# Attention and mixture of depths on one core: VectorE adds GpSimd's partial sum of probabilities, with another order of stores, PSUM banks and first halves

## The chip, the core and the metric

The kernel runs on one core of a Trainium2 chip. The metric is device time in microseconds (us), the median of several executions; smaller is better. The engines of the core work side by side, each on its own queue of instructions: TensorE (PE: matmuls and transposes, its weight loads are PEld), VectorE (DVE), ScalarE (ACT), GpSimd (POOL) and SyncE (SP, which here only issues transfers). TensorE writes to PSUM, which has eight banks.

## What is computed

Two blocks follow each other, all in float32:

```python
# attention: batch 8, 12 heads, 448 tokens, 64 per head
q_n, k_n = (rmsnorm(q, g_q), rmsnorm(k, g_k))      # x / sqrt(mean(x*x) + 1e-6) * g
scores = (1 / sqrt(64)) * matmul(q_n, k_n.T)
attn = exp(scores - max(scores))
attn = attn / (sum(attn) + 1e-9)
x = matmul(attn, v)                                # then (8, 448, 12*64 = 768)

# mixture of depths, per batch b
scores = x[b] @ w_gate
top_idx = the 128 tokens with the highest scores
h = maximum(x[b, top_idx] @ w1, 0)                 # 768 -> 1024
ye = h @ w2                                        # 1024 -> 768
out[b] = x[b]; out[b, top_idx] += sigmoid(scores[top_idx])[:, None] * ye
```

## The kernel before

The 12 heads of a batch are worked off in 3 groups of 4, so there are 24 groups `n`, numbered over all batches. A group has two pairs of heads (`hh`) and two heads in each (`c`), and its keys come in NI = 7 blocks of 64; one block of one group is a unit `u`, of which there are 168. Scores are kept with the keys on the partitions, so that the sum over keys (the denominator of the softmax) is a sum over partitions and blocks.

The start: the array of TensorE is kept at work by transposes that nobody reads, while the first rows are squared (ScalarE), summed (VectorE) and raised to -1/2 (GpSimd).

```python
    ps = ps_moe.tile([128, 512], F32, tag="moe", name="warm_ps")
    for _ in range(26):
        nc.tensor.transpose(out=ps[:, 0:128], in_=ident, identity=ident)
    ...
    def sum_squares(n, i, sq):                     # i = 0: queries, 1: keys
        ss = sss.pop((n, i))
        for h in [slice(0, 1), slice(1, 2)] if (n, i) == (0, 0) else [slice(0, 2)]:
            nc.vector.tensor_reduce(out=ss[:, h], in_=sq[:, h], axis=AX.X, op=OP.add)
        rinv = norm_pool.tile([128, 2, NI], F32, name="rinv", bufs=8)
        nc.gpsimd.tensor_tensor(out=rinv, in0=ss, in1=neg_half, op=OP.pow)   # shapes cut
```

For groups 0 and 1 TensorE spreads the queries' factors over the partitions (28 small matmuls, `scale_q_early`), and VectorE multiplies the queries `qT` by them. For later groups the factors go to DRAM and come back as a row for all partitions:

```python
    def rows_out(n): ...   # rows (DRAM) <- rinv, SyncE's queue
    def rows_in(n): ...    # bc <- rows, two transfers on SyncE's queue
    def scale_q(n):        # qT = qT * gg * bc
        nc.vector.scalar_tensor_tensor(out=t, in0=t, scalar=gg, in1=bcs.pop(n), ...)
```

For each unit TensorE makes the scores in two banks out of four (`ps_sc`), ScalarE takes the exponential into `p`, and TensorE multiplies by the values into `av`. The sum of `p` over the blocks of a group is shared out, for the first two batches (n < 6, `by_pool`):

```python
    def add_probs(u):
        n, i = divmod(u, NI)
        if i == NI - 1 and sums_last(n):           # block 6 is left for TensorE
            lasts.setdefault(n, []).append(probs.pop(u))
            return
        first = 2 if by_pool(n) else 0
        if first and i == 1:                       # blocks 0 and 1: GpSimd
            t = first_tokens[n % 2]...
            nc.gpsimd.tensor_tensor(out=t, in0=probs.pop(u - 1), in1=probs.pop(u), op=OP.add)
            lasts[n] = [t]
        elif i > first:                            # blocks 2 to 5: VectorE
            ...
            nc.vector.tensor_tensor(out=sums[n], in0=... , in1=probs.pop(u), op=OP.add)

    def sum_keys(n):
        ps = aux([128, 512], "den_ps")
        terms = [sums.pop(n)] + lasts.pop(n, [])   # n < 6: sum, GpSimd's sum, block 6
        for t in terms:
            for hh in range(2):
                for odd in range(2):
                    nc.tensor.matmul(out=ps[...], lhsT=pick_pair, rhs=..., start=..., stop=...)
```

`invert_sums` transposes the denominators and VectorE takes their reciprocal (`rden`); `to_tokens` transposes the result (`x_ps`) and VectorE multiplies by `rden` into `x`. After the third group of a batch come the gates, the store of `x`, and the ranks of the tokens:

```python
    def score_rows(b):
        ps = aux([128, 512], "row_ps")             # aux: one bank, which den_ps and x_ps use too
        for j in range(NJ):
            nc.tensor.transpose(out=ps[...], in_=t[:, j, :], identity=...)
        nc.scalar.copy(out=rows, in_=ps[:CP, 0:S])
```

```python
        at(s, gate, n)                             # in last_tokens; a slot s is one unit
        at(s, store_x, b)                          # out <- x, 1344 KB, SyncE's queue
        at(s + 1, spread, b)
        ...                                        # in ranks_of
        at(s + 2, select, b)                       # selected (DRAM) <- x, GpSimd's queue
        at(s + 8 if s >= 0 else s + 3, load_selected, b)   # xe <- selected, SyncE's queue
```

The two layers of batch b (`moe_ps`, on the 128 selected tokens `xe`) are then worked off between the units of later groups. A transfer waits at its place in SyncE's queue until what it needs is there, and those behind it wait too.

Of the kernel before, what the change touches and what calls it, by code (L numbers as in the profile page):

```python
# [10 lines left out]
F32 = mybir.dt.float32  # L11
I32 = mybir.dt.int32
AF = mybir.ActivationFunctionType
OP = mybir.AluOpType
# [11 lines left out]
class Loads:  # L26
# [37 lines left out]
    def get(self, name, n, i=None):  # L64
        return self.tiles[name, n, i]
# [3 lines left out]
def fast(  # L69
# [21 lines left out]
    nc = tc.nc  # L91

    B, NP, _, S = loads.src["qT"].shape
    CP = 112
    NJ = S // CP
    D = 64
    NI = S // D
# [14 lines left out]
    norm_pool = ctx.enter_context(tc.tile_pool(name="norm", bufs=2))  # L112
# [7 lines left out]
    ps_sc = ctx.enter_context(tc.tile_pool(name="ps_sc", bufs=4, space=PSUM))  # L120
# [6 lines left out]
    def aux(shape, name):  # L127

        if PER * now[0] >= units:
            return ps_sc.tile(shape, F32, tag="sc", name=name)  # L130
        if spare[0]:
            return ps_moe.tile(shape, F32, tag="moe", name=name)
        return ps_aux.tile(shape, F32, tag="aux", name=name)
# [7 lines left out]
    load, get, neg_half = loads.load, loads.get, loads.neg_half  # L141

    ident = const.tile([128, 128], F32, name="ident")
# [12 lines left out]
    for c in range(2):  # L156
        nc.vector.memset(pick_pair[D * c : D * (c + 1), c : c + 1], 1.0)
    nc.vector.scalar_tensor_tensor(
        out=gg, in0=loads.gcol[:, 0:1], scalar=scale, in1=loads.gcol[:, 1:2], op0=OP.mult, op1=OP.mult
    )  # L160

    ps = ps_moe.tile([128, 512], F32, tag="moe", name="warm_ps")
    for _ in range(26):
        nc.tensor.transpose(out=ps[:, 0:128], in_=ident, identity=ident)  # L164

    wg = const.tile([CP, DM], F32, name="wg")
# [43 lines left out]

    def sum_squares(n, i, sq):
        ss = sss.pop((n, i))
        for h in [slice(0, 1), slice(1, 2)] if (n, i) == (0, 0) else [slice(0, 2)]:
            nc.vector.tensor_reduce(out=ss[:, h], in_=sq[:, h], axis=AX.X, op=OP.add)  # L214
        rinv = norm_pool.tile([128, 2, NI], F32, name="rinv", bufs=8)
        flat = "p h i -> p (h i)"
        nc.gpsimd.tensor_tensor(  # L217
            out=rinv.rearrange(flat),
            in0=ss.rearrange(flat),
            in1=neg_half.to_broadcast([128, 2 * NI]),  # L220
            op=OP.pow,
        )
        rinvs[n, i] = rinv

    def rows_out(n):
# [26 lines left out]
    def scale_q_early(n):  # L252

        rinv = rinvs.pop((n, 0))
        for c in range(2):
            ps = ps_sc.tile([128, 512], F32, tag="sc", name="sc")
            r = slice(D * c, D * (c + 1))
            for i in range(NI):
                for hh in range(2):
                    nc.tensor.matmul(  # L260
                        out=ps[D * hh : D * (hh + 1), D * i : D * (i + 1)],
                        lhsT=rinv[r, hh, i : i + 1].to_broadcast([D, D]),
                        rhs=ident[r, r],
                        start=True,
                        stop=True,
                    )
            t = get("qT", n)[:, c].rearrange("d (p i) -> d p i", i=NI)
            nc.vector.scalar_tensor_tensor(  # L268
                out=t,
                in0=t,  # L270
                scalar=gg,
                in1=ps[:, 0:S].rearrange("d (i p) -> d p i", i=NI),
                op0=OP.mult,
                op1=OP.mult,
            )
# [3 lines left out]
    probs, sums, avs, xTs, rdens, xs = {}, {}, {}, {}, {}, {}  # L279
# [41 lines left out]
    def add_probs(u):  # L321
        n, i = divmod(u, NI)
        if i == NI - 1 and sums_last(n):
# [3 lines that stand above are left out]
        if first and i == 1:  # L327
            t = first_tokens[n % 2].rearrange("p h i d -> p h (i d)")
            nc.gpsimd.tensor_tensor(out=t, in0=probs.pop(u - 1), in1=probs.pop(u), op=OP.add)
            lasts[n] = [t]  # L330
        elif i > first:
            begins = i == first + 1
            if begins:
                sums[n] = p_pool.tile([128, 2, S], F32, name="sum", bufs=2)
            nc.vector.tensor_tensor(  # L335
                out=sums[n], in0=probs.pop(u - 1) if begins else sums[n], in1=probs.pop(u), op=OP.add
            )

    def values_out(n):
        for c in (1, 0):  # L340
            t = norm_pool.tile([128, NJ, CP], F32, name="xT", bufs=4)
            nc.scalar.copy(out=t.rearrange("d j p -> d (j p)"), in_=avs[n][c][:, 0:S])
            xTs[n, c] = t
        avs.pop(n)

    dens, lasts = {}, {}

    first_tokens = [get("tok", 0, i) for i in range(2)]

    def sums_last(n):  # L350


        return n < 2 * NG or n == n_groups - 1

    def by_pool(n):

        return n < 2 * NG
# [41 lines left out]
    def to_tokens(n, c):  # L399
        b = n // NG  # L400
        if b not in xs:
            xs[b] = x_pool.tile([CP, NJ, DX], F32, name="x")
        t = xTs.pop((n, c))
        shape = [128, NJ, 128]
        if c == 1 and not before_layers(now[0]):
            ps = ps_sc.tile(shape, F32, tag="sc", name="x_ps")
        else:
            ps = aux(shape, "x_ps")
        for j in range(NJ):
            nc.tensor.transpose(out=ps[:CP, j, :], in_=t[:, j, :], identity=ident)  # L410
        col = (n % NG * 2 + c) * 128
        nc.vector.tensor_tensor(  # L412
            out=xs[b][:, :, col : col + 128].rearrange("p j (h d) -> p j h d", d=D),
            in0=ps[:CP].rearrange("p j (h d) -> p j h d", d=D),
            in1=rdens[n][:, :, :, c, None].to_broadcast([CP, NJ, 2, D]),
            op=OP.mult,
        )
# [42 lines left out]

    def score_rows(b):
        t = rowss[b]
        ps = aux([128, 512], "row_ps")
        for j in range(NJ):
            nc.tensor.transpose(
                out=ps[:CP, CP * j : CP * (j + 1)], in_=t[:, j, :], identity=ident[:CP, :CP]
            )
        rows = moe_pool.tile([CP, S], F32, name="score_rows")
        nc.scalar.copy(out=rows, in_=ps[:CP, 0:S])
        nc.scalar.activation(out=parts[b], in_=parts[b], func=AF.Exp)  # L470
        rowss[b] = rows
# [162 lines left out]
    def at(slot, fn, *args):  # L634
        todo.setdefault(slot, []).append(lambda: fn(*args))

    now = [0, 0]
# [29 lines left out]
    for n in range(1, n_groups):  # L667
# [4 lines left out]
        if n > 1:  # L672
# [3 lines left out]
            first = max(s0 - (20 if n > 5 else 17), 0)  # L676
# [7 lines left out]
    def finish(n, q):  # L684

        if n == n_groups - 1:
            for fn, args in ((sum_keys, (n,)), (invert_sums, (n,)), (to_tokens, (n, 0))):
                task((q, 1), fn, *args)
            task((q, 1), last_tokens, n)
            return  # L690
        task((q, 1), sum_keys, n)
        task((q + 1, 0), to_tokens, n, 0)
        task((q + 1, 1), last_tokens, n)
# [7 lines left out]
    def before_layers(q):  # L701
        return done == 0 and ready.get(0, q + 1) > q

    def soon():

        q, place = now
        return PER * q + 2 * place if PER * q < units else -9

    def last_tokens(n):
        to_tokens(n, 1)  # L710
        b, g = divmod(n, NG)
        s = soon()
        at(s, gate, n)
        if g < NG - 1:
            return
        at(s, store_x, b)
        at(s + 1, spread, b)
        q, place = now

        when = (q + 1 + place // 2, 0) if b < B - 1 else (q + 1, 1)  # L720
        tasks.insert(0, (when, lambda: ranks_of(b)))

    def ranks_of(b):
        score_rows(b)
        s = soon()
        at(s, count, b, (0, 1))
        at(s + 1, count, b, (2, 3))
        at(s + 2, annotate, b)
        at(s + 2, select, b)
        at(s + 8 if s >= 0 else s + 3, load_selected, b)  # L730
        ready[b] = max((s + 8) // PER + 1, first_ff(b) - 1 if b else 0) if b < B - 1 else 0

    def first_ff(b):


        return -(-(units + 2 * PER - NG * NI * (B - 2 - b)) // PER)

    def run_values(upto, q):
        ended = False
        while waiting and waiting[0] <= upto:  # L740
            u = waiting[0]
            if ended and u % NI == 0:

                return
            values(waiting.pop(0))
            if u % NI == NI - 1:
                values_out(u // NI)
                finish(u // NI, q)
                ended = True
            add_probs(u)  # L750

    for i in range(2):
        sum_squares(0, i, squares(0, i))
    later = [squares(1, i) for i in range(2)]
    scale_q_early(0)
    for i in range(2):
        sum_squares(1, i, later[i])
# [587 lines left out]
```

## Time and profile before

| what | value |
|---|---|
| time, median of 3 runs | 530.28 us (528.81 to 530.87) |
| span of the profiled execution | 526.9 us |
| scores, 1344 matmul records | 154.8 us, 549 ns each |
| values, 1344 matmul records | 147.1 us, 537 ns each |
| denominators on GpSimd's sum (`den_ps<-tok`), 48 records | 3.4 us, 352 ns each |
| `sum<-sum,p` on VectorE, 128x896, 101 | 111.6 us, 1105 ns each |
| GpSimd's sum (`tok<-p`), 6 | 12.9 us, 2145 ns each |
| GpSimd's pow (`rinv<-ss`), 128x14, 48 | 128.8 us, 2689 ns each |
| out_dram<-x, 8 stores | 1344 KB each, 7.8 us from issue to landing (median) |

Records of matmuls overlap each other, up to four 64x64 parts of the array working at once, so the sums of their durations say less than the distance from one start to the next. A matmul of the program has two records. The wait view sums, for each instruction, the idle time of its engine just before it and names what ended it; the timeline lists instructions by start.

### The profile page before, as it was taken

To read this page: it belongs to the slowest core of one execution; us is meant where nothing else is said; L and a number is where in the kernel's file an instruction comes from. 1 tells how busy PE (TensorE), PEld (TensorE's weight loads), DVE (VectorE), ACT (ScalarE), POOL (GpSimd) and SP (SyncE) were. 2 spreads that over 40 slices of the span, in tenths; PEclk is the share of its full clock that TensorE was granted. 3 is DMA by queue.
4 is the path that set the end of the run, shared out by engine and by line. 5 is a ranking of instruction groups with operands and counts; after the bars stand their busy time and mean duration, and the time that the engine had idled before them with its cause. 6 is when DMAs were issued, how large, how long until landed. Compare 5 with 4: busy or idle time off the path is not lost.

```text
span 526.9 us, 11121 instructions
## 1 busy us (share of the span) xinstructions
PE 507.6 (96%) x4482; PEld 298.8 (57%) x4482; DVE 334.2 (63%) x638; ACT 278.1 (53%) x507; POOL 191.8 (36%) x109
## 2 busy tenths in 40 slices
PE   6999997999999999999999999998999999999995
PEld 5544343565744476546654467644664448659694
DVE  4566879579846896658666787467947487336101
ACT  4886873857644845456644585645463474401100
POOL 4956866623512454132712424304621003002102
PEclk9999998999999999999999999999999999999998
DMA  8968779799764297526846396537542231104100
GB/s 304 382 217 291 244 224 345 251 291 340 200 187 161 82 291 232 163 94 192 260 136 183 87 297 211 159 103 223 195 131 71 70 136 31 31 1 143 53 32 35
DMA packets 43405, 93.21 MB, mean 177 GB/s; under 512 B 11059, under 2 KB 23348, under 8 KB 43346
## 3 DMA queue, kind: packets, MB, share of 16 engines
q1 hardware_dynamic: 39938, 86.11, 52.1%
q0 software_dynamic: 3264, 6.31, 3.5%
q8 instruction: 37, 0.61, 0.5%
q14 instruction: 22, 0.18, 0.1%
q10 hardware_dynamic: 144, 0.00, 0.0%
HBM read 74.93 MB, written 25.35 MB: 190 GB/s over the span
## 4 chain that ended last, share of the span: by engine, by line
PE 89%; DVE 4%; DMA 2%; ACT 2%; issue 2%; POOL 0%; DVEq 0%; SPq 0%; ACTq 0%; POOLq 0%
PE sc L289 24%; PE av L313 22%; PE moe_ps L575 13%; PE moe_ps L595 11%; PE sc L595 4%; PE x_ps L410 4%; PE sc L575 4%; PE den_ps L367 3%; DMA bc<-rows 2%; PE denT_ps L392 1%; ACT p L298 1%; DVE sum L335 1%; PE warm_ps L164 1%; DVE ss L214 1%; DVE x L412 1%
## 5 line engine op out<-in xcount | busy, mean ns | idle before, releaser
L298 ACT ACTIVATE p<-sc,rinv 128x448 f32<-128x448 f32 x336 | 186.6, 642 | 106.3 <-PE sc L289 92.5
L217 POOL TENSOR_TENSOR rinv<-ss,neg_half 128x14 f32<-128x14 f32 x48 | 128.8, 2689 | 198.3 <-DVE ss L214 170.6
L289 PE MATMUL sc<-qT,kT 64*64 64x448 f32 x1344 | 154.8, 549 | 1.1 <-DVE qT L268 0.4
L313 PE MATMUL av<-p,v 64*64 64x448 f32 x1344 | 147.1, 537 | 0.0
L335 DVE TENSOR_TENSOR sum<-sum,p 128x896 f32<-128x896 f32 x101 | 111.6, 1105 | 7.2 <-ACT p L298 0.9
L313 PEld LDWEIGHTS av<-p,v 64*64 64x64 f32 x1344 | 60.1, 133 | 67.6 <-issue 56.9
L289 PEld LDWEIGHTS sc<-qT,kT 64*64 64x64 f32 x1344 | 54.3, 133 | 70.9 <-issue 47.0
L214 DVE TENSOR_REDUCE ss<-sq 128x14 f32<-128x910 f32 (+1 forms) x49 | 52.4, 1074 | 33.9 <-ACT sq L207 33.9
L575 PE MATMUL moe_ps<-xeT,w 128*128 128x128 f32 x576 | 69.3, 277 | 0.0
L575 PEld LDWEIGHTS moe_ps<-xeT,w 128*128 128x128 f32 x576 | 66.2, 192 | 5.3 <-issue 5.3
L595 PE MATMUL moe_ps<-w,hT 128*128 128x384 f32 x176 | 61.3, 491 | 0.4 <-DVE xe L604 0.3
L412 DVE TENSOR_TENSOR x<-x_ps,rden 112x512 f32<-112x512 f32 x48 | 32.8, 690 | 37.2 <-PE x_ps L410 36.4
L506 POOL DMA_INDIRECT selected<-x,rank x32 | 33.6, 1050 | 47.3 <-DVE x L498 39.3
L207 ACT ACTIVATE sq<-tok 128x896 f32<-128x896 f32 (+1 forms) x49 | 46.4, 951 | 5.7 <-DMA tok<-in_tok_dram 3.7
L595 PEld LDWEIGHTS moe_ps<-w,hT 128*128 128x128 f32 x176 | 31.7, 190 | 22.5 <-issue 2.5
L436 DVE SCALAR_TENSOR_TENSOR prod<-x,wg 112x256 f32<-112x256 f32 x96 | 41.5, 432 | 3.0
L614 POOL DMA_INDIRECT out_dram<-xe,row x10 | 11.6, 1164 | 81.1 <-DVE rden L394 47.3
L410 PE MATMUL x_ps<-ident,xT 128*112 128x128 f32 x192 | 29.5, 279 | 3.3 <-DVE rden L394 3.3
L335 DVE TENSOR_TENSOR sum<-p 128x896 f32<-128x896 f32 x24 | 25.9, 1078 | 5.2 <-ACT p L298 5.2
L604 DVE SCALAR_TENSOR_TENSOR xe<-sc,xe 128x384 f32<-128x384 f32 (+1 forms) x6 | 3.3, 550 | 40.6 <-PE sc L595 40.6
L410 PEld LDWEIGHTS x_ps<-ident,xT 128*112 128x112 f32 x192 | 21.8, 135 | 12.6 <-issue 7.7
L248 DVE SCALAR_TENSOR_TENSOR qT<-qT,gg,bc 128x896 f32<-128x896 f32 x22 | 25.2, 1147 | 5.1 <-DMA bc<-rows 5.1
(71 smaller groups left out, 311.0 us busy)
## 6 DMA issues: line engine op xcount, KB each, us to landing
tok<-in_tok_dram SPq DMA_DIRECT2D x48, 448.0 KB, 6.3
qT<-in_qT_dram SPq DMA_DIRECT2D x24, 448.0 KB, 6.2
kT<-in_kT_dram SPq DMA_DIRECT2D x24, 448.0 KB, 7.0
v<-in_vp_dram SPq DMA_DIRECT2D x24, 448.0 KB, 7.7
out_dram<-x SPq DMA_DIRECT2D x8, 1344.0 KB, 7.8
bc<-rows SPq DMA_DIRECT2D x44, 224.0 KB, 6.4
xe<-selected SPq DMA_DIRECT2D x8, 385.0 KB, 3.1
w<-in_moe_w_dram SPq DMA_DIRECT2D x6, 512.0 KB, 6.4
```

The source lines that it names most:

```text
L207: nc.scalar.activation(out=sq[:, h, :, 0:D], in_=t[:, h], func=AF.Square, scale=scale)
L214: nc.vector.tensor_reduce(out=ss[:, h], in_=sq[:, h], axis=AX.X, op=OP.add)
L217: nc.gpsimd.tensor_tensor(out=rinv.rearrange(flat), in0=ss.rearrange(flat), in1=neg_half.to_broadcast([128, 2 * NI]), op=OP.pow,)
L289: nc.tensor.matmul(out=scs[hh][D * c : D * (c + 1), 0:S], lhsT=get("kT", n)[r, c, D * i : D * (i + 1)], rhs=get("qT", n)[r, c, :], start=True,
L298: nc.scalar.activation(out=p[:, hh], in_=scs[hh][:, 0:S], func=AF.Exp, scale=rinvs[n, 1][:, hh, i : i + 1],)
L313: nc.tensor.matmul(out=avs[n][c][D * hh : D * (hh + 1), 0:S], lhsT=get("v", n)[r, hh, i, :], rhs=probs[u][r, hh], start=(i == 0), stop=(i ...
L335: nc.vector.tensor_tensor(out=sums[n], in0=probs.pop(u - 1) if begins else sums[n], in1=probs.pop(u), op=OP.add)
L410: nc.tensor.transpose(out=ps[:CP, j, :], in_=t[:, j, :], identity=ident)
L412: nc.vector.tensor_tensor(out=xs[b][:, :, col : col + 128].rearrange("p j (h d) -> p j h d", d=D), in0=ps[:CP].rearrange("p j (h d) -> p j ...
L436: nc.vector.scalar_tensor_tensor(out=prod, in0=xs[b][:, j, cols], scalar=1.0, in1=wg[:, cols], op0=OP.mult, op1=OP.mult, accum_out=gates[b ...
L575: nc.tensor.matmul(out=ps[:, 128 * i : 128 * i + n], lhsT=w1[:, dc, 128 * (f0 + i) : 128 * (f0 + i + 1)], rhs=xeT[:, dc, :n], start=(dc == 0),
L595: nc.tensor.matmul(out=ps[:n, :width], lhsT=hT[:, fc, :n], rhs=w2[:, fc, cols], start=(fc == 0), stop=(fc == NFC - 1),)
```

## The change

It has five parts.

- The transposes at the start are 13 instead of 26; for the first group the pow is taken by halves (one `hh` at a time), and the spreading matmuls go through both heads `c` of the first half before the second, so that they can begin with half of the factors.
- The sum that GpSimd makes of blocks 0 and 1 is added to `sums` by VectorE, after block 5, and TensorE no longer multiplies it into the denominators. It is meant to take work off TensorE.
- The score rows take a bank of the four of the scores instead of the one that they share with the denominators, once the layers have begun.
- The store of `x` is issued four units later, so that the row broadcasts and loads of later groups stand ahead of it in SyncE's queue.
- The load of the selected tokens is issued three units later, for the same reason.

```diff
-    for _ in range(26):
+    for _ in range(13):
         nc.tensor.transpose(out=ps[:, 0:128], in_=ident, identity=ident)
...
+        rinv = norm_pool.tile([128, 2, NI], F32, name="rinv", bufs=8)
         for h in [slice(0, 1), slice(1, 2)] if (n, i) == (0, 0) else [slice(0, 2)]:
             nc.vector.tensor_reduce(out=ss[:, h], in_=sq[:, h], axis=AX.X, op=OP.add)
-        rinv = norm_pool.tile([128, 2, NI], F32, name="rinv", bufs=8)
-        nc.gpsimd.tensor_tensor(out=rinv..., in0=ss..., in1=neg_half..., op=OP.pow)
+            nc.gpsimd.tensor_tensor(out=rinv[:, h]..., in0=ss[:, h]..., in1=neg_half..., op=OP.pow)
...  scale_q_early
-        for c in range(2):
-            ps = ps_sc.tile([128, 512], F32, tag="sc", name="sc")
-            for i in range(NI):
-                for hh in range(2):
-                    nc.tensor.matmul(out=ps[...], lhsT=rinv[r, hh, i : i + 1]..., rhs=ident[r, r], ...)
+        spreads = [ps_sc.tile([128, 512], F32, tag="sc", name="sc") for _ in range(2)]
+        for hh in range(2):
+            for c, i in [(c, i) for i in range(NI) for c in range(2)]:
+                nc.tensor.matmul(out=spreads[c][...], lhsT=rinv[r, hh, i : i + 1]..., rhs=ident[r, r], ...)
...  add_probs
-            lasts[n] = [t]
+            firsts[n] = t
...
+            if first and i == NI - 2:
+                nc.vector.tensor_tensor(out=sums[n], in0=sums[n], in1=firsts.pop(n), op=OP.add)
...  score_rows
-        ps = aux([128, 512], "row_ps")
+        if before_layers(now[0]):
+            ps = aux([128, 512], "row_ps")
+        else:
+            ps = ps_sc.tile([128, 512], F32, tag="sc", name="row_ps")
...
-        at(s, store_x, b)
+        at(s + 4 if s >= 0 else s, store_x, b)
...
-        at(s + 8 if s >= 0 else s + 3, load_selected, b)
+        at(s + 11 if s >= 0 else s + 3, load_selected, b)
```

More of the change, by code (lines that the diff above doesn't have):

```diff
@@ L212, in sum_squares @@
         ss = sss.pop((n, i))
+        rinv = norm_pool.tile([128, 2, NI], F32, name="rinv", bufs=8)
+        flat = "p h i -> p (h i)"
         for h in [slice(0, 1), slice(1, 2)] if (n, i) == (0, 0) else [slice(0, 2)]:
             nc.vector.tensor_reduce(out=ss[:, h], in_=sq[:, h], axis=AX.X, op=OP.add)
-        rinv = norm_pool.tile([128, 2, NI], F32, name="rinv", bufs=8)
[L216 to L222, printed above, removed]
+            nc.gpsimd.tensor_tensor(
+                out=rinv[:, h].rearrange(flat),
+                in0=ss[:, h].rearrange(flat),
+                in1=neg_half.to_broadcast([128, (h.stop - h.start) * NI]),
+                op=OP.pow,
+            )
         rinvs[n, i] = rinv
@@ L254, in scale_q_early @@
         rinv = rinvs.pop((n, 0))
-        for c in range(2):
-            ps = ps_sc.tile([128, 512], F32, tag="sc", name="sc")
-            r = slice(D * c, D * (c + 1))
-            for i in range(NI):
-                for hh in range(2):
[L260 to L266, printed above, removed]
+        spreads = [ps_sc.tile([128, 512], F32, tag="sc", name="sc") for _ in range(2)]
+        for hh in range(2):
+            for c, i in [(c, i) for i in range(NI) for c in range(2)]:
+                r = slice(D * c, D * (c + 1))
+                nc.tensor.matmul(
+                    out=spreads[c][D * hh : D * (hh + 1), D * i : D * (i + 1)],
+                    lhsT=rinv[r, hh, i : i + 1].to_broadcast([D, D]),
+                    rhs=ident[r, r],
+                    start=True,
+                    stop=True,
+                )
+        for c in range(2):
             t = get("qT", n)[:, c].rearrange("d (p i) -> d p i", i=NI)
@@ L271, in scale_q_early @@
                 scalar=gg,
-                in1=ps[:, 0:S].rearrange("d (i p) -> d p i", i=NI),
+                in1=spreads[c][:, 0:S].rearrange("d (i p) -> d p i", i=NI),
                 op0=OP.mult,
@@ L344, in values_out @@
         avs.pop(n)
-    dens, lasts = {}, {}
+    dens, lasts, firsts = {}, {}, {}
     first_tokens = [get("tok", 0, i) for i in range(2)]
```

## The prediction

> **What bounds the kernel now.** I read first the busy times of the page, then the idle time of TensorE by what ended it, then the stretches in which that idle time lies, in order of time.
>
> ```profile
> span 526.9 us, 11121 instructions
> PE 507.6 (96%) x4482; PEld 298.8 (57%) x4482; DVE 334.2 (63%) x638; ACT 278.1 (53%) x507; POOL 191.8 (36%) x109
> PEclk9999998999999999999999999999999999999998
> ```
>
> TensorE (PE) is the bound: busy 507.6 of 526.9 us. No other engine is near its limit over the whole span. So a change can pay in only three ways: take work off TensorE, shorten its 13 us of gaps (and the first instructions, 4.7 us in) and the end, or mend the one dip of its clock. The waits of TensorE name the gaps:
>
> ```profile
> PE warm_ps L164 <- DVE gg L158: 4.7, 1, 4.7
> PE x_ps L410 <- DVE rden L394: 3.3, 1, 3.3
> PE den_ps L367 <- ACT score_rows L469: 1.6, 2, 1.3
> PE den_ps L367 <- DVE sum L335: 1.4, 2, 1.2
> ```
>
> The columns are total us, times, longest. 3.3 us is one wait for VectorE, 1.4 us are two waits for its sum of probabilities, 1.6 us are two in which the denominators' PSUM bank was still held by the score rows. After 92 us TensorE's longest gap is 1.3 us.
>
> The 3.3 us gap lies in the slice in which the clock dips. The windows (us, busy of PE, PEld, DVE, ACT, POOL, granted clock, DMA share, GB/s) show the slice:
>
> ```profile
> 84.00:88.00 4.00, 0.74 (x4) 0.69 (x4) 3.69 (x6) 0.00 (x0) 3.50 (x3) 0.90 1.03 335
> 88.00:92.00 4.00, 4.00 (x30) 1.40 (x32) 3.86 (x11) 1.84 (x4) 3.38 (x4) 0.68 1.06 299
> ```
>
> The timeline of SyncE's queue, then that of VectorE (start, duration, line, operation, tiles; in brackets the idle time before it and what ended it):
>
> ```profile
> 69.62 0.69 SPq L424 DMA_DIRECT2D out_dram<-x  x1
> 70.83 0.47 SPq L239 DMA_DIRECT2D bc<-rows  x1
> ```
>
> ```profile
> 72.07 2.09 DVE L457 TENSOR_SCALAR parts<-gate 112x4 f32<-112x4 f32 x1
> 74.08 1.08 DVE L335 TENSOR_TENSOR sum<-sum,p 128x896 f32<-128x896 f32 x1
> ...
> 79.45 1.15 DVE L248 SCALAR_TENSOR_TENSOR qT<-qT,gg,bc 128x896 f32<-128x896 f32 x1 [2.35 <-DMA bc<-rows]
> ...
> 84.75 2.29 DVE L335 TENSOR_TENSOR sum<-sum,p 128x896 f32<-128x896 f32 x2
> 86.95 0.25 DVE L394 RECIPROCAL rden<-denT_ps 112x16 f32<-112x16 f32 x1
> ```
>
> SyncE's queue issues nothing from 62.94 to 69.62: it stands at the store of batch 0 (1344 KB), which waits for the last columns of x. The row broadcast bc stands behind it, goes out at 70.83 and lands at 79.4. VectorE waits 2.35 us for it, is otherwise full from 68.9 on, and reaches the reciprocal that TensorE needs 3.3 us late. TensorE then runs at half clock: (1-0.90)x4/0.5 + (1-0.68)x4/0.5 = 0.8 + 2.6 = 3.4 us of it.
>
> **What the Trainium skill says.** "TensorE: Matmul & The Clock Gate", Part 1: the array runs at half clock until a free-running window of about 3.4 us has been busy, and falls back after an idle one. The trace agrees: 3.4 us of half clock after a 3.3 us gap, and the warm-up transposes take 421 ns (median) at first and 272 ns at the end. "SBUF — State Buffer", Who interferes with whom: a VectorE instruction with two SBUF inputs and a GpSimd instruction that reads SBUF exclude each other for a whole instruction. The trace agrees: the sum at 34.33 took 2.80 us instead of 1.09 while GpSimd's sum ran from 33.75 to 36.18. "DMA: Bandwidth & Descriptors", Queues, rings and completion order: one issuing queue's descriptors are taken in ring order on each of the 16 engines, so bc, issued after a 1344 KB store, stands behind it; 8.5 us from issue to landing against a median of 6.4 agree.
>
> **The change part by part.** Minus is a gain.
>
> *Start.* The 26 warm-up transposes run from 4.67 to 9.64. While cold they start every 0.213 us (18 or so up to 8.5), so 13 end near 4.67 + 13x0.213 = 7.45. GpSimd's first pow, 128x14, runs 6.50 to 9.10, 2.6 us. Cut by halves of 128x7 I estimate 1.35 us each (2.6 over two, and a little fixed cost): the first can start when the first reduce is done, about 5.97, and ends near 7.3, the second near 8.7. The 28 spreading matmuls last 9.57 to 11.25, so half of them take 0.8 us warm, perhaps 1.6 cold. The first 14 now fill 7.45 to about 9.0, the second 14 end near 9.8 if the clock has risen, 10.5 if not. Both scalings of qT (0.65 us from start to start) now wait for the last of them, so the second ends near 11.1 or 11.8, instead of 11.98. Exponentials start 0.2 to 0.9 us sooner; their scale, the key's pow, is done by 11.3, no later. I take -0.6.
>
> *Denominators.* Six groups (two batches) lose their four matmuls on GpSimd's sum. In group 2 these start at 58.59 and the next at 58.97: 0.39 us with their neighbours. 6 x 0.39 = -2.3 of TensorE.
>
> *VectorE's extra add.* Six of 1.09 us, 6.6 us in the first 100 us. What counts is where TensorE waits for the result. Order of VectorE's queue: the add follows directly on the last sum. Groups 0 and 1: the sum is done some 4 us or more before the denominators, nothing lost. Group 2: TensorE already waits 1.16 us for it, +1.1. Group 3: it waits 0.28 us, +1.1. Group 4: the add lies directly ahead of the reciprocal at 86.95, +1.1 there. Group 5: 0.76 us of slack ahead of its reciprocal, then nearly nothing.
>
> *SyncE's order.* In the queue of the changed kernel bc precedes the store, so it can go out soon after 62.5, when the rows are written (5.4 us median), and lands well before 77. VectorE's 2.35 us wait goes: -2.35 at the reciprocal. load_selected, three slots later, frees the loads that stand behind it from 86.1 to 94.03, but these aren't waited for by TensorE, so I give it nothing.
>
> *Score rows in a score bank.* It applies once the layers run. The 1.3 us (at 366.1) and 0.3 us (at 306.9) of waiting go; the score bank is one of four, and its use shifts later scores by part of an exponential. -1.4.
>
> **The sum, along the gates.** Start -0.6, groups 0 and 1 -0.8: TensorE comes 1.4 us sooner to group 2, where the longer add takes 1.1 back and 0.4 is saved: -0.7. VectorE's full stretch begins with TensorE's x_ps at 67.3, so it begins 0.7 sooner; up to the reciprocal it loses 2.35 of waiting and gains 2x1.1 of adding, so the reciprocal comes 0.7+0.15 = 0.85 us sooner. TensorE, held at group 3 by its add, comes to that gate about as late as before, and waits some 2.4 us instead of 3.3. That is short enough that no whole window is idle: the half clock goes, which cost 1.1 us in the scores after it (2.85 instead of 1.73) and 0.5 in the transposes before them, -1.6. Now -2.45. Groups 4 and 5: -0.8. Score rows: -1.4. In all -4.65, and 530.28 - 4.65 = 525.6 us.
>
> **The rivals.**
> (1) *VectorE becomes the bound of the first 90 us.* For it: it is busy 3.6 to 3.9 of 4 us in most windows from 68 to 92, and each added sum has two SBUF inputs, so it may stand 1 to 2 us behind GpSimd. Against it: between 92 and 96 it is nearly idle and can catch up. If two adds collide and the half clock stays, the kernel ends at 528 to 530.
> (2) *The order of SyncE's queue is worth more than the wait that is seen.* With bc and the loads behind it sooner, ScalarE's squares and VectorE's reduces may also come sooner, and the 3.3 us gap may close to under 1 us: 523 to 524.
> (3) *The shorter warm-up leaves the first scores at half clock.* For it: half of 13 x 0.213 us is slack against a window of 3.4. Against it: the first spreading matmuls begin as the transposes end, so TensorE stays busy. It would cost 1 to 2 us: 527.
> (4) *Score banks.* If the scores after score_rows wait a whole exponential (0.64 us) in each of seven batches, the 1.4 us are gone: 527.
>
> **Range and chances.** Rivals 1, 3 and 4 push up by up to 3 us, rival 2 down by 2 to 3; the runs of before spread over 2 us. I predict 525.6 us, 522.5 to 528.8 for eight in ten. 2% would be 10.6 us; the gaps that the change touches and the matmuls that it removes sum to about 10 us only if nothing is paid for the adds. Faster by over 2% 0.02, within 2% 0.96, slower 0.02.
>
> **What would show it.** The first scores near 10.7 instead of 11.39; no den_ps<-tok; seven-element pows near 1.35 us; bc landed before the scaling of qT near 77, and no wait for it; a wait of 2 to 3 us for rden near 87, with the clock at full in both windows; a den_ps wait for the sum of about 2 us near 57; no den_ps wait for score_rows. The prediction is wrong if the clock dips again, if the den_ps waits stay under 1 us although the adds are there, or if new waits for banks appear in the layers.

## The result and the profile after

The changed kernel takes 526.82 us (median of 4 runs, 525.40 to 527.47) against 530.02 us of the kernel before on the same chip: ratio 0.9938, 95% interval 0.9909 to 0.9966. That is 3.2 us less, where the prediction had 4.65 us less (525.6 us, range 522.5 to 528.8). Measured again beside other kernels it gave 527.34 us and a ratio of 0.9958 (0.9940 to 0.9976).

The page of the kernel after, the lines that answer to those shown of before:

```profile
span 523.7 us, 10997 instructions
PE 504.8 (96%) x4421; PEld 295.6 (56%) x4421; DVE 340.2 (65%) x644; ACT 277.5 (53%) x507; POOL 193.1 (37%) x110
PEclk9999999999999999999999999999999999999998
```

TensorE is still the bound. VectorE has 6.0 us more (340.2 for 334.2), about what six adds of 1.09 us should bring. TensorE has 2.8 us less. The waits of TensorE in the kernel after (total us, times, longest):

```profile
PE den_ps L369 <- DVE sum L339: 3.9, 2, 2.1
PE sc L289 <- DVE qT L268: 1.9, 2, 1.1
PE x_ps L412 <- DVE rden L396: 0.5, 1, 0.5
```

L339 is the new add. The wait for the reciprocal (3.3 us before) is 0.5 us, the wait for the sum is 3.9 instead of 1.4 us, a wait for the scaling of qT has grown from 0.4 to 1.9 us, and no wait for the score rows is left in the list.

The windows round the old gap (us, busy of PE, PEld, DVE, ACT, POOL, granted clock, DMA share, GB/s), in the kernel after:

```profile
76.00:80.00 4.00, 3.78 (x32) 1.47 (x36) 3.93 (x11) 2.25 (x4) 0.00 (x0) 0.63 1.04 416
80.00:84.00 4.00, 4.00 (x44) 1.54 (x40) 3.72 (x9) 2.34 (x6) 2.82 (x2) 0.94 1.04 345
84.00:88.00 4.00, 3.46 (x34) 1.68 (x30) 3.79 (x6) 1.13 (x3) 3.39 (x3) 1.00 1.05 269
```

The half clock is not gone. It stands 10 us earlier, from 77 to 80.5: (0.37x4 + 0.06x4)/0.5 = 3.4 us of it. The timeline of TensorE in the kernel after shows what it does:

```profile
76.22 0.59 PE L369 MATMUL den_ps<-sum,pick_pair 128*32 128x224 f32 x8 [1.74 <-DVE sum L339]
...
77.11 3.27 PE L289 MATMUL sc<-qT,kT 64*64 64x448 f32 x16
...
85.19 0.60 PE L412 MATMUL x_ps<-ident,xT 128*112 128x128 f32 x4
86.33 0.65 PE L412 MATMUL x_ps<-ident,xT 128*112 128x128 f32 x4 [0.55 <-DVE rden L396]
```

TensorE waits 1.74 us for the added sum of group 3, falls to half clock, makes scores in 3.27 us that took 1.7 before, and so comes to the reciprocal almost as late as VectorE does. The timeline of VectorE up to there, in the kernel after:

```profile
73.88 1.08 DVE L335 TENSOR_TENSOR sum<-sum,p 128x896 f32<-128x896 f32 x1
75.07 1.09 DVE L339 TENSOR_TENSOR sum<-sum,tok 128x896 f32<-128x896 f32 x1
...
77.41 1.15 DVE L248 SCALAR_TENSOR_TENSOR qT<-qT,gg,bc 128x896 f32<-128x896 f32 x1
...
86.03 0.25 DVE L396 RECIPROCAL rden<-denT_ps 112x16 f32<-112x16 f32 x1
```

The scaling of qT is no longer kept waiting by bc (77.41 instead of 79.45), and the reciprocal is at 86.03 instead of 86.95. In the kernel before VectorE had also stood idle shortly ahead of its wait for bc; the kernel after has no such gap there:

```profile
75.60 0.69 DVE L479 SCALAR_TENSOR_TENSOR cmp<-score_rows,gate,earlier 112x448 f32<-112x448 f32 x1 [0.44 <-issue]
```

A useful ruler is the end of the last exponential of each group, read from ScalarE's timeline of one execution of each kernel. After minus before: group 1 -0.35 us, group 2 -0.75, group 3 -0.15, group 4 +2.32, group 5 -2.64, group 6 -2.82, then constant to group 18 (-2.83), and -3.5 from group 19 to the end. So nearly all that the change does happens in the first 100 us, and once more near 366 us. The spans differ by 3.2 us; the 0.2 us lost behind the last exponential were not traced.

### The profile page after: what moved, and what is told of

It is laid out like the page before. It is cut to its first block, busy times and chain, and to the rows that moved or that the text cites. A ratio compares the mean times of both kernels' runs of the same rounds, so it can differ in the third digit from the quotient of the medians.

```text
span 523.7 us, 10997 instructions
## 1 busy us (share of the span) xinstructions
PE 504.8 (96%) x4421; PEld 295.6 (56%) x4421; DVE 340.2 (65%) x644; ACT 277.5 (53%) x507; POOL 193.1 (37%) x110
## 4 chain that ended last, share of the span: by engine, by line
PE 87%; DVE 7%; DMA 4%; issue 1%; ACT 0%; SPq 0%; POOL 0%; DVEq 0%; POOLq 0%; ACTq 0%
PE sc L289 24%; PE av L313 22%; PE moe_ps L581 13%; PE moe_ps L601 11%; PE x_ps L412 4%; PE sc L601 4%; PE sc L581 4%; PE den_ps L369 3%; DMA tok<-in_tok_dram 2%; PE denT_ps L394 1%; DVE sum L335 1%; DVE prod L438 1%; DMA out_dram<-xe,row 1%; DVE x L414 1%; DMA qT<-in_qT_dram 1%
## 5 line engine op out<-in xcount | busy, mean ns | idle before, releaser
L217 POOL TENSOR_TENSOR rinv<-ss,neg_half 128x14 f32<-128x14 f32 (+1 forms) x49 | 128.3, 2623 | 194.1 <-DVE ss L216 162.0
L289 PE MATMUL sc<-qT,kT 64*64 64x448 f32 x1344 | 157.1, 550 | 2.2 <-DVE qT L268 1.9
L313 PE MATMUL av<-p,v 64*64 64x448 f32 x1344 | 149.3, 538 | 0.0
L335 DVE TENSOR_TENSOR sum<-sum,p 128x896 f32<-128x896 f32 x101 | 109.9, 1088 | 7.1 <-ACT p L298 0.7
L335 DVE TENSOR_TENSOR sum<-p 128x896 f32<-128x896 f32 x24 | 27.8, 1157 | 4.6 <-ACT p L298 4.6
L344 ACT COPY xT<-av 128x448 f32<-128x448 f32 x48 | 23.4, 549 | 8.3 <-PE av L313 7.8
L590 ACT ACTIVATE hT<-moe_ps 128x512 f32<-128x512 f32 x12 | 7.2, 597 | 38.3 <-PE moe_ps L581 38.3
```

What stands on the lines that cost most here:

```text
L217: nc.gpsimd.tensor_tensor(out=rinv[:, h].rearrange(flat), in0=ss[:, h].rearrange(flat), in1=neg_half.to_broadcast([128, (h.stop - h.start) ...
L289: nc.tensor.matmul(out=scs[hh][D * c : D * (c + 1), 0:S], lhsT=get("kT", n)[r, c, D * i : D * (i + 1)], rhs=get("qT", n)[r, c, :], start=True,
L313: nc.tensor.matmul(out=avs[n][c][D * hh : D * (hh + 1), 0:S], lhsT=get("v", n)[r, hh, i, :], rhs=probs[u][r, hh], start=(i == 0), stop=(i ...
L335: nc.vector.tensor_tensor(out=sums[n], in0=probs.pop(u - 1) if begins else sums[n], in1=probs.pop(u), op=OP.add)
```

## The experiments

Medians below stand beside the kernel before in the same job; the ratio is to it, with its 95% interval. The ratio lies nearer to that of the averages than to that of the medians, so that it and the medians can differ by some tenths of a per cent.

**Each part alone.** The first four kernels are the kernel before (529.6 us) with one part of the change.

The new start alone (13 transposes, pow by halves, order of the spreading matmuls, as in the diff above).

> The kernel before with the new start alone (13 transposes, pow by halves, the order of the spreading matmuls). Theory: the first exponentials come 0.7 us sooner (near 12.4 instead of 13.1 us), but the loads of tok for group 2 land at the same 17.6 us, VectorE reduces them ahead of the second scaling of qT, and TensorE waits for that scaling about 1.1 us near 19.3 instead of 0.4: end unchanged, 530.0 us (within 0.2). Rival: the 0.6 us stay to the end, 529.4 us.

Measured: 529.55 us, ratio 0.9998 (0.9985 to 1.0010). The end is unchanged as the theory has it, but the interval reaches from 0.8 us less to 0.5 us more, so that the rival's 0.6 us aren't excluded; the mechanism is only half shown. The start does what it should: in the kernel after the first scores begin at 10.72 instead of 11.39. Then the path runs over the loads. The timeline of the kernel after:

```profile
17.66 0.96 ACT L207 ACTIVATE sq<-tok 128x896 f32<-128x896 f32 x1 [0.79 <-DMA tok<-in_tok_dram]
18.71 1.10 DVE L216 TENSOR_REDUCE ss<-sq 128x14 f32<-128x910 f32 x1 [5.43 <-ACT sq L207]
19.73 1.26 DVE L268 SCALAR_TENSOR_TENSOR qT<-qT,gg,sc 128x448 f32<-128x448 f32 x2
20.46 1.19 PE L289 MATMUL sc<-qT,kT 64*64 64x448 f32 x5 [1.12 <-DVE qT L268]
```

tok of group 2 lands at 17.6 us, ScalarE squares it, VectorE reduces it ahead of the scaling that TensorE waits for. These scores began at 20.42 before. In the profile of b_start the same load was a little earlier and TensorE waited only 0.38 us: there 0.6 us were kept to the end. In the nine profiles of kernels with the new start and the old order of reduces the wait is 0.20 to 2.02 us (0.25 in a_again, 2.02 in a_part_sel9, both below). So the gain is there or not as the loads land, and on the average of 14 runs none is resolved.

VectorE's add alone:

```diff
-            lasts[n] = [t]
+            firsts[n] = t
...
+            if first and i == NI - 2:
+                nc.vector.tensor_tensor(out=sums[n], in0=sums[n], in1=firsts.pop(n), op=OP.add)
```

> The kernel before with VectorE's add of GpSimd's sum alone. Theory: groups 0 and 1 gain 0.4 us each; group 2 waits 2.2 us for the sum instead of 1.2; two adds lie ahead of the reciprocal near 87 us, which comes about 2.2 us later than before less 0.1; groups 4 and 5 gain 0.4 each: about 1.3 us slower, 531.3 us. Rival: TensorE's 2.3 us less work count and the adds are hidden, 527.7 us.

Measured: 529.75 us, ratio 1.0000 (0.9987 to 1.0014). Both were wrong: no loss of 1.3 us, no gain of 2.3. Its profile, which is of the fastest of its runs (527.63 us), shows the two waits of 2.14 and 1.74 us for the sum, as expected. But the add of group 3 is taken up ahead of bc: the scaling of qT starts at 79.33 instead of 79.45, its wait for bc is 1.94 us instead of 2.35, and 0.44 us in which VectorE stood idle at 75.2 are gone. So the reciprocal comes 1.0 us later, not 2.2. And the half clock has moved, which was in neither theory:

```profile
77.01 3.20 PE L289 MATMUL sc<-qT,kT 64*64 64x448 f32 x16
...
88.26 0.65 PE L412 MATMUL x_ps<-ident,xT 128*112 128x128 f32 x4 [2.51 <-DVE rden L396]
88.84 1.74 PE L289 MATMUL sc<-qT,kT 64*64 64x448 f32 x16
```

It runs from 77.1 to 80.6 us, behind the wait for the sum, and not from 87.2 to 90.6 as before. So group 5 ends 0.71 us sooner than before although the reciprocal is later. Why the 14 runs gain nothing on average isn't shown by this one profile.

SyncE's order alone (both `s + 4` for the store and `s + 11` for the selected tokens):

> The kernel before with the later store of x and the later load of the selected tokens alone. Theory: VectorE no longer waits 2.35 us for bc, the wait of TensorE for the reciprocal near 84 to 87 us falls from 3.3 to about 1 us and the half clock after it goes: 3.9 us less, 526.1 us. Rival: a wait or a dip of the clock takes the place of the one removed, 1 to 2 us less, 528.5 us.

Measured: 529.89 us, ratio 0.9995 (0.9979 to 1.0011). The theory's time is wrong, and so is the rival's, which had the kind right (a wait takes the place of the one removed) and neither its place nor its size. VectorE's timeline shows the theory's first half right: the scaling of qT at 76.82 without a wait, the reciprocal at 84.31 instead of 86.95. Group 5 ends 4.00 us sooner than before. Then the profile of b_store has this:

```profile
103.70 0.58 PE L547 MATMUL moe_ps<-ident,xe 128*128 128x128 f32 x3 [3.59 <-DMA xe<-selected]
104.08 1.05 PE L410 MATMUL x_ps<-ident,xT 128*112 128x128 f32 x4
104.92 0.85 PE L547 MATMUL xeT_ps<-ident,xe 128*128 128x128 f32 x3
105.70 0.97 PE L367 MATMUL den_ps<-sum,pick_pair 128*32 128x224 f32 x8
```

TensorE waits 3.6 us for the selected tokens of batch 0, then works at half clock (denominators 0.97 instead of 0.58 us). Group 6 ends 1.4 us later than before. SyncE's queue shows why: xe now stands behind bc and the loads ahead of it.

```profile
94.00 1.09 SPq L239 DMA_DIRECT2D bc<-rows  x2
95.14 0.58 SPq L524 DMA_DIRECT2D xe<-selected  x1
```

Issued at 95.14 it lands at 103.65, 8.5 us later; the busy share of the 16 transfer engines is 0.91 from 92 to 104 us. In the kernel before it went out at the head of the queue and landed 2.8 us later (share 0.77):

```profile
94.03 0.34 SPq L524 DMA_DIRECT2D xe<-selected  x1
```

No run has the later store with the load of xe at its old place; the last three kernels below, with the load one unit later, come nearest.

The score rows in a score bank alone:

> The kernel before with the score rows in a score bank alone. Theory: only the wait of 1.3 us near 366 us goes, and half of it comes back as scores that wait for ScalarE's copies: 0.7 us less, 529.3 us. Rival: both waits go whole, 1.6 us less, 528.4 us.

Measured: 528.84 us, ratio 0.9985 (0.9974 to 0.9995), 0.8 us less (0.3 to 1.4). As the theory has it; the rival's 1.6 us lie outside. In its profile the gain is a step of 0.7 us between groups 18 and 19; near 306 us nothing is gained, since the scores that follow there wait for ScalarE's copies instead.

**Parts taken out of the full change** (beside 530.62 us before).

TensorE multiplies GpSimd's sum as before, all else as changed:

> The changed kernel with GpSimd's sum left to TensorE as before. Theory: TensorE has 2.3 us more of work, but its waits for the sum near 56 and 74 us fall by 1.1 us each, the half clock near 77 us goes, and VectorE reaches the reciprocal near 86 us 2.2 us sooner: 1.5 us less than the changed kernel, 525.3 us. Rival: the add is a gain as meant, 1 to 2 us more than the changed kernel, 528 us.

Measured: 531.21 us, ratio 0.9987 (0.9967 to 1.0007); its runs fall in two bunches, 526.1 to 529.9 and 530.8 to 533.9. Both wrong. TensorE's waits in a_noadd:

```profile
PE moe_ps L551 <- DMA xe<-selected: 4.9, 1, 4.9
PE den_ps L367 <- DVE sum L335: 1.4, 2, 1.2
PE x_ps L410 <- DVE rden L394: 1.3, 1, 1.3
```

The waits for sum and reciprocal fall as the theory said, and group 5 ends 3.83 us sooner than before. Then TensorE waits 4.9 us for xe (the profile is of a run of the upper bunch, 531.6 us). SyncE's queue in a_noadd, then in the kernel after:

```profile
95.25 1.09 SPq L239 DMA_DIRECT2D bc<-rows  x2
96.39 0.58 SPq L528 DMA_DIRECT2D xe<-selected  x1
```

```profile
90.69 1.09 SPq L239 DMA_DIRECT2D bc<-rows  x2
94.04 0.33 SPq L530 DMA_DIRECT2D xe<-selected  x1
```

TensorE would have come to xe at 100.3 us; in the kernel after it comes at 101.45. That is 1.2 us of the 4.9. The larger part is the transfer: in a_noadd bc goes out 11.3 us after the store of its rows was issued, in the kernel after 7.1, and xe behind it lands at 105.1 instead of 101.4.

The add in groups 0, 1 and 5 alone:

```diff
-            firsts[n] = t
+            if n in (0, 1, 5):
+                firsts[n] = t
+            else:
+                lasts[n] = [t]
...
-            if first and i == NI - 2:
+            if n in firsts and i == NI - 2:
```

> The changed kernel with VectorE's add in groups 0, 1 and 5 alone, where VectorE has slack, and TensorE's four matmuls in groups 2, 3 and 4. Theory: as without any add, and 3 times 0.39 us less: 2.7 us less than the changed kernel, 524.1 us. Rival: VectorE isn't the bound there and the add was a gain: 1 us more, 527.8 us.

Measured: 530.02 us, ratio 0.9983 (0.9964 to 1.0001): the same miss, with 3.4 us of waiting for xe near 100 us and 3.86 us gained up to group 5.

Transposes that keep the clock up in the wait of group 3:

```diff
+        if n == 3:
+            keep = ps_moe.tile([128, 512], F32, tag="moe", name="keep_ps")
+            for _ in range(14):
+                nc.tensor.transpose(out=keep[:, 0:128], in_=ident, identity=ident)
         terms = [sums.pop(n)] + lasts.pop(n, [])
```

> The changed kernel with 14 transposes that nobody reads, ahead of the denominators of group 3 (near 74.5 us), while TensorE waits for the sum. Theory: the clock stays at full, the scores near 77 us take 1.7 instead of 3.3 us, but the reciprocal near 86 us comes from VectorE, whose queue is not moved, so that TensorE only waits about 2 us there instead of 0.5: end unchanged within 0.3 us, 526.8 us. Rival: the half clock was on the path, 1.5 us less, 525.3 us.

Measured: 528.41 us, ratio 0.9970 (0.9949 to 0.9992), by its interval neither better nor worse than the changed kernel, so the rival's gain of 1.5 us isn't seen, though the wait for xe named below could hide one. The timeline of a_keep carries the theory:

```profile
76.44 1.73 PE L289 MATMUL sc<-qT,kT 64*64 64x448 f32 x16
...
85.58 0.65 PE L416 MATMUL x_ps<-ident,xT 128*112 128x128 f32 x4 [2.10 <-DVE rden L400]
86.16 2.79 PE L289 MATMUL sc<-qT,kT 64*64 64x448 f32 x14
```

With the clock up the scores take 1.73 us, and TensorE waits 2.10 us for the reciprocal instead of 0.55. The reciprocal is at 85.27 instead of 86.03, and 0.70 of these 0.76 us were gained by the end of group 2 already. So the half clock from 77 to 80.5 costs next to nothing: VectorE sets the time of 86 us. (In this execution the clock fell after that second wait, and xe was waited for, 3.3 us.)

VectorE's first reduce for group 2 behind the second scaling of qT:

```diff
-            at(slot + 2 * i + 1, lambda i=i: sum_squares(n, i, sq.pop(i)))
+            late = 2 if (n, i) == (2, 0) else 1
+            at(slot + 2 * i + late, lambda i=i: sum_squares(n, i, sq.pop(i)))
```

> The changed kernel with VectorE's first reduce for group 2 behind the scaling of qT for group 1 instead of ahead of it. Theory: the 1.1 us wait of TensorE near 19.3 us goes, and 0.7 to 1.1 us of it stay up to group 2, whose denominators then wait longer only if VectorE's stretch doesn't move: 0.8 us less, 526.0 us. Rival: the next loads hold the same scores back, no change, 526.8 us.

Measured: 528.17 us, ratio 0.9957 (0.9925 to 0.9989, 8 runs). Inconclusive. The wait at 19 us is gone in its profile, but in that execution the spreading matmuls lasted from 7.79 to 10.94, most of it at half clock, so the first scores began only at 11.71.

**The load of the selected tokens** (beside 529.75 us before, the last kernel beside 529.68). First the changed kernel itself once more:

> The changed kernel unaltered, to stand beside the next two on the same chip. Theory (the load of the selected tokens, xe, now stands behind the row broadcast in SyncE's queue and lands late whenever the transfers near 85 to 95 us run late): its times spread from 525 to 531 us from run to run, median near 528, while the kernel before stays near 530. Rival: it is steady near 526.8 us.

Measured: 527.34 us, ratio 0.9958 (0.9940 to 0.9976), 525.3 to 532.5. The theory's spread is there, by three of 19 runs above 529 us; the median lies between the theory's 528 and the rival's 526.8. Its waits:

```profile
PE den_ps L369 <- DVE sum L339: 3.9, 2, 2.1
PE x_ps L412 <- DVE rden L396: 2.2, 1, 2.2
PE sc L289 <- DVE qT L268: 1.0, 2, 0.8
PE moe_ps L553 <- DMA xe<-selected: 0.6, 1, 0.6
```

The same program now has no half clock near 77 us, waits 2.2 us for the reciprocal, and takes the same span (523.6 us): it says of the half clock what a_keep says, and more plainly. And 0.6 us of waiting for xe, which the first profile didn't have, shows how near the edge that load is.

xe one unit later than before instead of three, so that it stands ahead of kT, v and bc:

```diff
-        at(s + 11 if s >= 0 else s + 3, load_selected, b)
+        at(s + 9 if s >= 0 else s + 3, load_selected, b)
```

> The changed kernel with the load of xe one unit later than before instead of three, so that it stands ahead of kT, v and bc in SyncE's queue. Theory: xe always lands before TensorE needs it near 100 us; 526 us with a spread as small as that of the kernel before, about 1 to 2 us under the changed kernel. Rival: SyncE's queue stands at xe and the loads behind it come late, same as the changed kernel or slower.

Measured: 526.91 us, ratio 0.9928 (0.9898 to 0.9958), 524.7 to 527.9 over 7 runs. No wait for xe is left in the profile and the spread is as small as expected; a gain over the changed kernel (0.4 us of the medians) isn't resolved.

The same with the add in groups 0, 1 and 5 alone:

> The changed kernel with VectorE's add in groups 0, 1 and 5 alone and xe loaded one unit later than before. Theory: without the wait for xe the 3.9 us that the same kernel with the late load had gained up to group 5 stay, and 0.7 us of the score rows and 0.4 us of group 5 come to them: 5 us under the kernel before, 525 us. Rival: another transfer takes the place of xe: no more than 3 us under it, 527 us.

Measured: 524.34 us, ratio 0.9887 (0.9855 to 0.9918). This beats both kernels. The edit from a_part is the one line above; the 3.4 us wait is gone and the gain stays: group 5 ends 3.10 us sooner than before, the last group 3.87. SyncE's queue in a_part_sel9:

```profile
96.20 0.33 SPq L533 DMA_DIRECT2D xe<-selected  x1
```

That is as late as in a_noadd (96.39), so it isn't the moment of issue that counts. The queue had issued nothing for 5.7 us ahead of it, and TensorE finds xe landed when it comes at 100.84.

And with no add at all:

> The changed kernel without any add on VectorE (TensorE multiplies GpSimd's sum as before) and with xe loaded one unit later than before. Theory: what separates it from the kernel with the add in groups 0, 1 and 5 is 3 times 0.39 us of TensorE: 1.2 us more than that one, 525.5 us, ratio to before 0.991. Rival: the add helps nowhere, and it equals that one, 524.3 us.

Measured: 524.66 us, ratio 0.9910 (0.9890 to 0.9930). It equals a_part_sel9 within the intervals, so whether the add helps where VectorE has slack stays open. That it doesn't help in groups 2, 3 and 4 together is shown: with it everywhere and the same load (a_sel9) the kernel takes 526.91 us, and the averages of a_sel9 and a_part_sel9 in one job are 526.5 and 524.4 us.

## Why the prediction was right, and where it was not

The range held and the direction too. By its own steps, with the ruler's numbers of one profile of each kernel:

- *Start, -0.6*: the first half was right (first scores at 10.72, predicted near 10.7; each half pow 1.49 us, predicted 1.35), the step to the end failed in the kernel after: the next tok load took it back. Alone it isn't resolved in 14 runs.
- *Denominators, -0.39 each*: right, -0.35 and then -0.75 at groups 1 and 2.
- *The add, +1.1 in group 2*: right; TensorE waits 2.14 us, "about 2 us" predicted. In group 3 it waits 1.74, where 0.28 + 1.1 was worked out.
- *SyncE's order at the reciprocal*: the mechanism was right; bc went out at 66.3 and wasn't waited for. That the reciprocal came 0.92 us sooner, where 0.85 was predicted, is in part luck. VectorE's last sum of group 3 began only 0.20 us sooner (73.88 for 74.08), not 0.7, since the gain of the start was lost. And the two adds cost 1.8 us, not 2.2, since VectorE was not "full from 68.9 on"; in the kernel before it stood idle 0.44 us ahead of 75.60 (the line stands in the section on the result). Along VectorE's queue: 0.20 sooner, 0.68 later by the add of group 3, 2.52 sooner without the wait for bc, 1.12 later by the add of group 4.
- *The half clock, -1.6, and the wait of 2.4 us that remains*: the sum was right and the picture half wrong. I took for granted that a wait too short for an idle window keeps the clock, and named a new dip as a sign of being wrong; it came. The 1.74 us wait at 74.5 was enough to lose the clock, and the wait that remained was 0.55 us. But that dip lay in front of a gate that VectorE sets (the reciprocal at 86 us, for which TensorE has to wait in any case), so it cost next to nothing, and after the gate the clock was full, which is where it counts: group 5 at -2.64, against -2.45 and -0.39 for group 4, -2.84 predicted. In a_again the picture came out as well: no dip, and a wait of 2.2 us. b_add shows that the add alone can move the dip ahead of the gate, b_store that SyncE's order alone removes it there.
- *Score rows, -1.4*: mis-sized. b_rows gives -0.8: the 1.3 us wait went, scores behind it took half back, and the 0.3 us wait was no gain.
- *The load of the selected tokens, "I give it nothing"*: this step failed, and it was the one that mattered for what the change could have been. I asked what stands behind it in the queue and not what now stands ahead of it. Without the add the late load costs most of what the new order brings (ratio 0.9987 against 0.9910 with the load two units sooner, 0.8%, some 4 us). In the changed kernel's two profiles it costs nothing and 0.6 us. By these ratios the adds help beside the late load (0.9987 becomes 0.9938 or 0.9958) and not beside the earlier one (0.9910 becomes 0.9928). So what the trade of VectorE's time for TensorE's brought seems to have been a shorter wait for xe. How it shortened it is shown in part only: TensorE comes to xe some 1.2 us later with the adds, but xe also lands earlier, and why it does isn't shown. In a_keep, which has all the adds, it landed late and was waited for.

By the ruler the profile lacks 0.2 us of the prediction at group 5, another 0.2 at group 6, 0.7 at the score rows and 0.2 behind the last exponential: together the difference between 4.65 and 3.2, within rounding. The lost 0.6 us of the start don't show in this sum, since VectorE's gap stood in for them.

"SBUF — State Buffer", Who interferes with whom, of the Trainium skill, explains one more line of the kernel after. A small copy of VectorE, 0.39 us before, took 2.28 us (start 71.55) while GpSimd's sum ran from 71.48 to 73.57. The page names copies among the operations that can shut GpSimd out and be shut out; the trace agrees.

## What to carry to other kernels

When a transfer is moved back in a queue, look at both sides: what it lets pass, and how long it now has before its reader comes, with that reader moved forward by everything else in the change. Before work is moved from the bound engine to one with a low average load, ask whether that engine has slack at the moment of use; here the adds in three of six places together cost some 2 us (a_sel9 against a_part_sel9). The loss of clock ahead of the gate that VectorE sets cost next to nothing here, so find such gates before counting one. And check a predicted time at several points on the way: here two errors nearly cancelled at the reciprocal.

## What was not expected of the hardware

The clock of TensorE fell after a gap of 1.74 us with small transposes and 32-column matmuls round it, not only after gaps of 3.3 us; each time it stayed at half for 3.4 us. So the rule that the prediction took over, that a whole idle window is needed, doesn't hold for this trace. Whether it falls differs between executions of one program: the changed kernel has a dip from 77 to 80.5 us in one profile and none in the other, with spans of 523.7 and 523.6 us; a_sel9 lost the clock behind its wait of 2.1 us for the sum of group 2 (half from 59.1 to 62.5 us), the changed kernel behind the like wait didn't. GpSimd's pow took 1.49 us for 7 elements in each partition and 2.57 for 14 in the kernel after, so halving it saves 1.1 us of 2.6.
